# Pooled attention with a feed-forward layer: the maximum over partitions spread by one bfloat16 product, scales made straight from PSUM

## The chip, the cores and the metric

The kernel runs on one core of a Trainium2 chip, as one program. The metric is the device time of one execution in microseconds; lower is better. A core has a matrix engine (TensorE, PE), a vector engine (VectorE, DVE), an activation engine (ScalarE, ACT), a general engine (GpSimd, POOL) and a queue engine (SyncE, SP). They run side by side and meet through semaphores. TensorE writes to PSUM, an accumulator memory of 8 banks; the rest lies in SBUF. TensorE's weight loads are shown apart as PEld.

## The reference

There are 4 batches of 8 heads, 1152 positions and 64 values per head. Queries are averaged in pairs along the sequence, so that 576 query rows attend to 1152 keys. The result goes through a layer with normalisation and two products of 512 x 2048 and 2048 x 512.

```python
q_pool = q.reshape(B, H, S // 2, 2, D).mean(axis=3)
scores = scale * np.matmul(q_pool, k.transpose(0, 1, 3, 2))
scores = scores - np.max(scores, axis=-1, keepdims=True)
attn = np.exp(scores)
attn = attn / (np.sum(attn, axis=-1, keepdims=True) + 1e-09)
x = np.matmul(attn, v)          # then heads side by side: (4, 576, 512)
mu = np.mean(x, axis=-1, keepdims=True)
var = np.mean((x - mu) ** 2, axis=-1, keepdims=True)
xn = (x - mu) / np.sqrt(var + 1e-06) * g_ln
out = x + np.maximum(xn @ w_ch1, 0.0) @ w_ch2
```

All inputs and the output are float32.

## The kernel before

Two heads of one batch make a pair; there are 16 pairs, and each has 9 steps of 128 query rows (144 steps in all, `step(i)`). The order of the work is written out by hand: `step` emits for each engine what it does in step `i`, and a few queues (`reds`, `found`, `evacs`, `preps`, `units`, `calm`, and `todo` and `early` by step number) hold work that is slipped in between.

A float32 product is made out of float16 products: a matrix is scaled by a power of two and split into a high and a low float16 part. For this the kernel needs a bound of the largest absolute value of k, q and v of each pair and of each of four weight parts. `bound` (or `w_reduce` for weights) leaves one value on each of the 128 partitions; `all_max` makes the maximum over the partitions and spreads it to all of them; `scales` (or `w_scales`) makes powers of two out of it by masking exponent bits. All of this happens 20 times: once ahead of the first step, once for each of the pairs 1 to 15 (in step 3 of the pair before), and four times for weights.

`all_max` has two halves. `one` (L204) transposes the column of values, so that 1 to 3 rows of 128 values lie in PSUM; VectorE takes their maximum (L207) and puts it on the diagonal of a tiny matrix `dg` (L208). `two` (L215) multiplies a float32 matrix of ones of 3 rows by 128 columns with `dg`, so that each partition holds the maxima in PSUM. Then `scales` (L235 to L249) runs on VectorE: copy out of PSUM with a least bound TINY, mask the exponent (L240), mask and invert it (L241), multiply the inverse by 2^13 (L243), and make the product of two exponents `sc` (L245, L249). `w_scales` (L765 to L778) is the same for a weight part.

Steps 0 to 35 (batch 0, to about 186 us) transpose the exponentials on TensorE in float32 (`emit_t`, L431; `emit_t_copy`, L437) and multiply them in float32 (L455), while the weights are loaded and converted on VectorE (L103 in the profile). There `two` follows `emit_t` on TensorE, and what VectorE does with its result follows the step's maximum (L384). In the later steps (L365 and L373 are the scores, L467 the product with v, L619 and L651 the feed-forward products) the exponentials are split into `hl` (L412; the low part on VectorE, L421, or on GpSimd in every third step, L254 and L419) and transposed by DMA. There the results of `all_max` are taken in `flush`, in line with the other evacuations of PSUM: L516 and L517 (the sums of a row), L632 and L633 (the feed-forward's first layer: ScalarE writes the high part, VectorE the low part and frees the bank), L289 and L286 (the transposed k and q, which need the new scale `s`).

GpSimd adds the pairs of query rows (`pool_q`, L166) for two pairs at once, as soon as their DMA has landed; it also splits the weights (`w_split_a`, `_b`, `_c`: L254 and L797) and v (`take_v`).

The lines that a reader needs beside the functions printed below are these.

```python
# step(), steps of the first batch
emit_t(i)
if reds:
    found.append(reds.popleft()())
# step(), later steps
red = reds.popleft(); put = [None]
until([lambda: put[0]()])      # taken in the next flush()
...
put[0] = red()                 # after the product with v
```

Of the kernel before, what the change touches and what calls it, by code (L numbers as in the profile page):

```python
# [9 lines left out]
FP32 = mybir.dt.float32  # L10
FP16 = mybir.dt.float16
BF16 = mybir.dt.bfloat16
I32 = mybir.dt.int32
ACTF = mybir.ActivationFunctionType
ALU = mybir.AluOpType
# [3 lines left out]
EXPO = 0x7F800000  # L19
SIGN = -0x80000000  # L20
TINY = 2.0 ** -80
# [3 lines left out]
def tile_pooled_attention_moe(  # L25
# [18 lines left out]
    nc = tc.nc  # L44
# [18 lines left out]
    const = ctx.enter_context(tc.tile_pool(name="const", bufs=1))  # L63
# [5 lines left out]
    sm_p = ctx.enter_context(tc.tile_pool(name="sm", bufs=2))  # L69
# [4 lines left out]
    psum = ps_p.tile([128, 8, 512], FP32, name="psum")  # L74


    ident = const.tile([128, 128], FP32, name="ident")
# [3 lines left out]
    gsb = const.tile([128, KD], FP32, name="gsb")  # L81
    gs1 = const.tile([128, 2, KD], FP32, name="gs1")
    wtop = const.tile([128, 4, KD, 2], FP32, name="wtop")
    ones3 = const.tile([3, 128], FP32, name="ones3")
    wmax = const.tile([128, 4], FP32, name="wmax")
    wexp = const.tile([128, 4], FP32, name="wexp")
    wscl = const.tile([128, 4], FP32, name="wscl")
    inv12 = const.tile([128, 2], FP32, name="inv12")
    both = const.tile([128, 2], FP32, name="nhalf")
# [18 lines left out]
    def load(p, which, eng):  # L108
        b, hp = divmod(p, HP)
        h = 2 * hp  # L110
        src = k if which == "k" else v
        x = src[b, h:h + 2].rearrange("h (p c) d -> p h c d", c=C)
        if which == "k":
            r = raw_p.tile([128, 2, C + 1, D], FP32, tag="kr", name="kr")
            eng.dma_start(out=r[:, :, 0:C], in_=x)
            eng.dma_start(out=r[:, :, C], in_=x[:, :, C - 1])
        else:
            r = raw_p.tile([128, 2, C, D], FP32, tag="vr", name="vr")
            eng.dma_start(out=r, in_=x)
        raws[p, which] = r  # L120

    def load_q(p, engs, us=(0, 1)):

        if 0 in us:
            r = raw_p.tile([128, 2, C, 2, D], FP32, tag="qr", name="qr", bufs=2)
        else:
            r = raws[p, "q"]
        for u in us:
            b, hp = divmod(p + u, HP)
            for h in range(2):  # L130
                engs[(2 * u + h) % len(engs)].dma_start(
                    out=r[64 * u:64 * u + 64, h],
                    in_=q[b, 2 * hp + h].rearrange("(p c r) d -> p c r d", c=C, r=2),
                )
            raws[p + u, "q"] = r
# [3 lines left out]
    def state(p):  # L139
        if p not in pair:  # L140
            pair[p] = {
                x: sm_p.tile([128, 3], FP32, tag=x, name=x, bufs=3)
                for x in ("acc", "red", "e", "s", "sc")
            }
        return pair[p]

# [45 lines left out]

    def all_max(src, n, then):

        mx = sm_p.tile([3, 1], FP32, tag="mx3", name="mx3")
        dg = sm_p.tile([3, 3], FP32, tag="dg", name="dg")

        def place():
            u = this[0] if on_pe(this[0]) else pv_slot[0]
            return psum[:, 3 * (u % 2) + 2, 258:386]  # L200

        def one():
            ps = place()
            nc.tensor.transpose(ps[0:n], src, ident)  # L204

            def evac():
                nc.vector.tensor_reduce(mx[0:n], ps[0:n], axis=AX.X, op=ALU.max)  # L207
                nc.vector.scalar_tensor_tensor(  # L208
                    dg[0:n, 0:n], ps[0:n, 0:n], mx[0:n], ident[0:n, 0:n], op0=ALU.max, op1=ALU.mult
                )  # L210
            return evac

        def two():
            ps = place()
            nc.tensor.matmul(out=ps[:, 0:n], lhsT=ones3[0:n], rhs=dg[0:n, 0:n], start=True, stop=True)  # L215
            return lambda: then(ps[:, 0:n])

        return one, two


    reds, found = deque(), deque()

    def scales_reduce(p, a=0, b=3, then=None):
        def end(ps):
# [3 lines left out]

        reds.extendleft(reversed(all_max(pair[p]["acc"][:, a:b], b - a, end)))

    def scales(p, top, a=0, b=3, both=False):
        st = pair[p]
        red, e, s, sc = (st[x] for x in ("red", "e", "s", "sc"))
        v = nc.vector
        v.tensor_scalar(red[:, a:b], top, TINY, None, op0=ALU.max)  # L235
        if both:

            v.tensor_tensor(red[:, 0:1], red[:, 0:1], red[:, 2:3], op=ALU.max)
        ri, ei, si = (x.bitcast(I32)[:, a:b] for x in (red, e, s))
        v.tensor_scalar(ei, ri, EXPO, None, op0=ALU.bitwise_and)  # L240
        v.tensor_scalar(si, ri, EXPO, EXPO, op0=ALU.bitwise_and, op1=ALU.bitwise_xor)  # L241

        v.tensor_scalar(s[:, a:b], s[:, a:b], 2.0 ** 13, None, op0=ALU.mult)  # L243
        if a == 0:
            v.scalar_tensor_tensor(  # L245
                sc[:, 0:1], e[:, 0:1], 2.0 ** -32, e[:, 1:2], op0=ALU.mult, op1=ALU.mult
            )
            if on_pe(p * C):
                v.scalar_tensor_tensor(  # L249
                    sc[:, 1:2], e[:, 0:1], -(2.0 ** -32), e[:, 1:2], op0=ALU.mult, op1=ALU.mult  # L250
                )

    def scaled(dst, src, s=1.0):
# [85 lines left out]
    def on_pe(i):  # L339

        return 0 <= i < HP * C
# [196 lines left out]
    free_banks = [6, 7]  # L538
# [222 lines left out]

    def w_scales(part, top):
        w = part // 2
        m, e, s = wmax[:, part:part + 1], wexp[:, part:part + 1], wscl[:, part:part + 1]
        nc.vector.tensor_scalar(m, top, TINY, None, op0=ALU.max)  # L765
        mi = m.bitcast(I32)
        nc.vector.tensor_scalar(e.bitcast(I32), mi, EXPO, None, op0=ALU.bitwise_and)
        nc.vector.tensor_scalar(
            s.bitcast(I32), mi, EXPO, EXPO, op0=ALU.bitwise_and, op1=ALU.bitwise_xor
        )  # L770

        nc.vector.tensor_scalar(s, s, 2.0 ** (3 if part % 2 == 0 else 13), None, op0=ALU.mult)
        if part % 2 == 0:
            nc.vector.tensor_scalar(gs1[:, w], gsb, s, None, op0=ALU.mult)
        else:
            nc.vector.scalar_tensor_tensor(  # L778
                inv12[:, w:w + 1], wexp[:, part - 1:part], 2.0 ** -20, e,
                op0=ALU.mult, op1=ALU.mult,  # L780
            )

# [32 lines left out]
    for p in range(1, NP):  # L815
# [4 lines left out]
        if p % 2 == 0:  # L820
# [4 lines left out]
            else:  # L825
                x = i0 - (6 if p == 6 else 5)
# [234 lines left out]
    def warm(n, ps=None):  # L1061
        ps = psum[:, 2, 0:128] if ps is None else ps[:, 0:128]
        for _ in range(n):
            nc.tensor.matmul(out=ps, lhsT=ident16, rhs=ident16, start=True, stop=True)

    with tc.manual_schedule():
        def now(fn, *a, **k):
            fn(*a, **k)

        load_q(0, (nc.sync, nc.scalar), (0,))  # L1070
        load(0, "k", nc.sync)
        load(0, "v", nc.scalar)
        load_q(0, (nc.sync,), (1,))
        nc.sync.dma_start(out=gsb, in_=g_ln.rearrange("(k p) -> p k", p=128))
        nc.vector.memset(nhalf, -0.5)
        nc.vector.memset(both[:, 1:2], 0.0)
        nc.vector.memset(both[64:65, 1:2], 1e-9)
        nc.vector.memset(ones3, 1.0)
        nc.scalar.activation(out=wexp[:, 0:1], in_=nhalf, func=ACTF.Exp)
        make_identity(nc, ident)  # L1080

        warm(110)
        st = state(0)
        nc.vector.memset(st["acc"], 0.0)
        lower = (0, 64)
        pool_q(0, nc.vector, (lower,))
        dup_q(0, nc.gpsimd, (lower,))
        bound(0, "q", *lower)

        nc.scalar.activation(  # L1090
            out=kt_of(0).rearrange("p a h n -> p (a h n)")[:, 0:C * D],
            in_=raws[0, "k"][:, 0, 0:C].rearrange("p c d -> p (c d)"), func=ACTF.Abs,
            accum_out=st["acc"][:, 0:1],
        )
        nc.vector.tensor_reduce(
            st["acc"][:, 2:3], raws[0, "k"][:, 1, 0:C], axis=AX.XY, op=ALU.max,
            apply_absolute_value=True,
        )
        one, two = all_max(st["acc"], 3, lambda ps: scales(0, ps, 0, 3, both=True))
        one()()  # L1100
        two()()
        free_banks[:] = [6, 7, 3, 4, 5]
        parts = [fn(0, u) for fn, u in PREPS[:3]]
        for hi, lo in parts:
            hi()
            lo()
        warm(16)
        emit_s(0)
        preps.extend((fn, 0, u) for fn, u in PREPS[3:])
        free_banks[:] = [6, 7]  # L1110
        for h in range(2):
            take_v(0, h)
        i = 0
        while i < NSTEP + 20 or units or evacs or norms:
            step(i)
            i += 1
# [29 lines left out]
```

## Time and profile before

| what | value |
|---|---|
| time, median of 3 runs | 838.04 us (836.68 to 840.03) |
| span of the profiled execution | 836.1 us |
| PE busy | 808.8 us, 97% of the span |
| PEld busy | 575.8 us, 69% |
| DVE busy | 608.3 us, 73% |
| ACT busy | 558.0 us, 67% |
| POOL busy | 352.0 us, 42% |
| chain that ended last | PE 72%, DVE 10%, ACT 9%, DMA 4% |

The span runs from the first to the last instruction of one profiled execution. No time of its own is given for that execution beside the span; the three timed runs lie 0.6 to 3.9 us above it, their median 1.9 us. Busy time is what an engine spent in instructions. The chain follows the work that ended last back to what released each step. "Issue" in it is time in which an engine waited for nothing that the profile shows.

### The profile page before, as it was taken

Reading aid. Unit: us, or ns where it says so; the run is one execution under the profiler, and the core shown is the slowest. Engines: PE = TensorE matmul, PEld = TensorE weight load, DVE = VectorE, ACT = ScalarE, POOL = GpSimd, SP = SyncE. Lnnn points to the kernel's source line nnn. Section 1 sums busy time; section 2 is a strip of 40 time slices with the busy share of each in tenths; the row PEclk is TensorE's granted clock in tenths of the full one; section 3 lists DMA queues with packets and bytes.
Section 4 is the critical chain, followed back from the end, with each engine's and each line's share of the span. In section 5 each row is a group of like instructions: output and inputs, shape, how many; then the busy total and the mean of one; then the engine's idle time right before and its main releaser. Section 6 shows DMA issues by size and latency. Waiting matters only on the chain.

```text
span 836.1 us, 21671 instructions
## 1 busy us (share of the span) xinstructions
PE 808.8 (97%) x9142; PEld 575.8 (69%) x9142; DVE 608.3 (73%) x1167; ACT 558.0 (67%) x810; POOL 352.0 (42%) x343
## 2 busy tenths in 40 slices
PE   8999999998899989999999999999999999999997
PEld 6787887777566666767576766766666767667764
DVE  3598989899788888897887778888787877522221
ACT  3999988976787868787776777677867766211110
POOL 3020334287999972356452543636243432200000
PEclk9999999999999999999999999999999999999999
DMA  6954474115698989899979987996969867401001
GB/s 162 249 175 139 157 209 161 32 60 114 131 186 136 192 160 199 144 189 180 183 135 179 208 162 140 177 204 104 212 118 194 144 119 137 89 2 26 15 1 25
DMA packets 276018, 115.97 MB, mean 139 GB/s; under 512 B 259280, under 2 KB 259280, under 8 KB 275920
## 3 DMA queue, kind: packets, MB, share of 16 engines
q1 hardware_dynamic: 275568, 113.70, 66.0%
q8 instruction: 71, 1.16, 0.6%
q10 hardware_dynamic: 352, 0.88, 0.4%
q14 instruction: 27, 0.22, 0.1%
HBM read 46.14 MB, written 4.72 MB: 61 GB/s over the span
## 4 chain that ended last, share of the span: by engine, by line
PE 72%; DVE 10%; ACT 9%; DMA 4%; issue 3%; POOL 2%; SPq 1%; ACTq 0%; POOLq 0%; DVEq 0%
PE psum L651 21%; PE psum L619 21%; PE psum L467 10%; PE psum L365 8%; ACT pe L398 3%; PE psum L373 3%; DVE mx L384 3%; PE psum L455 2%; PE psum L328 2%; PE psum L431 2%; DVE hl L421 1%; PE psum L300 1%; ACT pt L437 1%; DMA kr<-in_k_dram 1%; DMA stage<-in_moe_w_ch_dram 1%
## 5 line engine op out<-in xcount | busy, mean ns | idle before, releaser
L384 DVE TENSOR_REDUCE mx<-psum 128x1 f32<-128x1152 f32 x144 | 194.3, 1349 | 16.4 <-PE psum L467 6.8
L398 ACT ACTIVATE pe<-psum,nb,sc 128x1152 f32<-128x1152 f32 x144 | 188.5, 1309 | 21.8 <-POOL hl L419 9.3
L651 PE MATMUL psum<-wsl,ht 128*128 128x512 f16 x864 | 196.7, 379 | 0.2 <-ACT pe L398 0.2
L619 PEld LDWEIGHTS <-wsl 128*128 128x128 f16 x1920 | 170.7, 98 | 23.2 <-issue 3.9
L619 PE MATMUL psum<-xn,wsl 128*128 128x256 f16 x1536 | 179.0, 275 | 3.5 <-DVE ht L633 2.3
L651 PEld LDWEIGHTS <-ht 128*128 128x128 f16 x864 | 80.5, 98 | 88.3 <-issue 0.2
L365 PE MATMUL psum<-kt,qt 64*128 64x512 f16 (+1 forms) x960 | 127.2, 380 | 4.8 <-ACT pe L398 4.5
L632 ACT ACTIVATE ht<-psum 128x512 f16<-128x512 f32 x72 | 42.9, 596 | 132.3 <-PE psum L619 132.1
L412 ACT ACTIVATE hl<-pe 128x1152 f16<-128x1152 f32 x108 | 125.6, 1163 | 3.4
L467 PE MATMUL psum<-vt,pt 128*128 128x65 f16 (+1 forms) x3240 | 117.7, 194 | 0.4 <-DMA pt<-hl 0.2
L421 DVE SCALAR_TENSOR_TENSOR hl<-pe,hl 128x1152 f16<-128x1152 f32 x72 | 112.2, 1559 | 0.0
L467 PEld LDWEIGHTS <-pt 128*128 128x128 f16 (+1 forms) x3240 | 109.2, 100 | 3.3 <-DMA pt<-hl 0.7
L254 POOL TENSOR_SCALAR pe<-pe 128x1152 f32<-128x1152 f32 x36 | 43.4, 1205 | 142.1 <-ACT hl L412 142.1
L633 DVE SCALAR_TENSOR_TENSOR ht<-psum,ht 128x512 f16<-128x512 f32 x72 | 49.6, 689 | 73.6 <-ACT ht L632 73.6
L419 POOL TENSOR_TENSOR hl<-pe,hl 128x1152 f16<-128x1152 f32 x36 | 85.5, 2374 | 3.0
L455 PE MATMUL psum<-pt,vt 128*65 128x128 f32 (+1 forms) x720 | 77.3, 262 | 1.0 <-DVE qt L286 1.0
L455 PEld LDWEIGHTS psum<-pt,vt 128*65 128x65 f32 x720 | 71.6, 138 | 1.1 <-DVE qt L286 1.1
L365 PEld LDWEIGHTS <-qt 64*128 64x128 f16 (+1 forms) x960 | 39.7, 96 | 42.5 <-issue 25.9
L373 PEld LDWEIGHTS <-qt 128*128 128x128 f16 (+1 forms) x320 | 17.1, 99 | 62.0 <-issue 61.8
L286 DVE SCALAR_TENSOR_TENSOR qt<-psum,s,qt 128x384 f16<-128x384 f32 x48 | 29.5, 615 | 34.8 <-ACT qt L289 34.6
L260 POOL COPY gate<-gate 128x1 f32<-128x1 f32 x27 | 5.2, 191 | 111.0 <-DVE gate L259 111.0
L665 DVE SCALAR_TENSOR_TENSOR xb<-psum,inv,xb 128x512 f32<-128x512 f32 x32 | 23.8, 745 | 36.9 <-PE psum L651 36.8
(117 smaller groups left out, 1025.7 us busy)
## 6 DMA issues: line engine op xcount, KB each, us to landing
stage<-in_moe_w_ch_dram SPq DMA_DIRECT2D x32, 512.0 KB, 5.8
kr<-in_k_dram SPq DMA_DIRECT2D x16, 576.0 KB, 4.4
qr<-in_q_dram SPq DMA_DIRECT2D x31, 288.0 KB, 6.0
vr<-in_v_dram SPq DMA_DIRECT2D x15, 576.0 KB, 4.8
out_dram<-xb SPq DMA_DIRECT2D x32, 128.0 KB, 2.5
pt<-hl SPq DMA_TRANSPOSE x108, 4.9
kr<-in_k_dram SPq DMA_DIRECT2D x16, 64.0 KB, 4.1
vr<-in_v_dram ACTq DMA_DIRECT2D x1, 576.0 KB, 7.6
```

The lines of the kernel that those rows point to most:

```text
L254: nc.gpsimd.tensor_scalar(dst, src, s, 1.0, op0=ALU.mult, op1=ALU.mult)
L365: nc.tensor.matmul(out=sp[o:o + w, c0:c0 + 512], lhsT=qt[r:r + 64, qa, q0:q0 + w], rhs=kt[r:r + 64, ka, h], start=(a == 0), stop=(a == 2),)
L384: nc.vector.tensor_reduce(mx, st["s"], axis=AX.X, op=ALU.max)
L398: nc.scalar.activation(out=st["pe"], in_=st["s"], func=ACTF.Exp, scale=pair[i // C]["sc"][:, 0:1], bias=st["nb"],)
L412: nc.scalar.activation(out=hl[:, 0], in_=st["pe"], func=ACTF.Copy, scale=2.0 ** 15)
L419: nc.gpsimd.tensor_tensor(hl[:, 1], st["pe"], hl[:, 0], op=ALU.subtract)
L421: nc.vector.scalar_tensor_tensor(hl[:, 1], st["pe"], 2.0 ** 15, hl[:, 0], op0=ALU.mult, op1=ALU.subtract)
L455: nc.tensor.matmul(out=ps[0:65, q0:q0 + w], lhsT=vt[:, h, c], rhs=pt[:, 128 * u + q0:128 * u + q0 + w], start=(u == 0), stop=(u == C - 1),)
L467: nc.tensor.matmul(out=dst[:, 0:n], lhsT=lhsT, rhs=rhs, start=(u == 0 and lhsT is hi and n == 65), stop=(u == C - 1 and lhsT is lo), skip_ ...
L619: nc.tensor.matmul(out=ps[:, o:o + n], lhsT=wsl[:, 8 * w + cc, wa, f * 128:f * 128 + 128], rhs=xn[:, xa * KD + cc, 0:n], start=(m == 0), s ...
L633: lambda: nc.vector.scalar_tensor_tensor(lo, pv, 0.0, hi, op0=ALU.max, op1=ALU.subtract),
L651: nc.tensor.matmul(out=ps, lhsT=hv[0][:, ha, f, t * 128:t * 128 + 128], rhs=wsl[:, 8 * w + 4 + f // 2, wa, (f % 2) * DM:(f % 2) * DM + DM] ...
```

## The change

`two` multiplies a bfloat16 matrix of 128 x 128 equal values (2^-13) with a bfloat16 matrix `dg` of 128 rows, of which all but the diagonal of the first rows is zero. `dg` is one of four places of a constant tile that is zeroed once. The least bound TINY is written once into one PSUM column (386) of banks 2 and 5, next to the 128 columns that `one` fills, and L207 reduces 129 columns. `scales` and `w_scales` mask exponents straight out of PSUM; the copy with TINY and the multiplication by 2^13 are gone, their factors are in other constants. Ahead of the first step the maximum of two parts of k is taken before the transpose, not after it.

```diff
-    ones3 = const.tile([3, 128], FP32, name="ones3")
+    ones = const.tile([128, 128], BF16, name="ones")
+    diag = const.tile([128, 4, 4], BF16, name="diag")
...
     def all_max(src, n, then):
         mx = sm_p.tile([3, 1], FP32, tag="mx3", name="mx3")
-        dg = sm_p.tile([3, 3], FP32, tag="dg", name="dg")
+        diags[0] += 1
+        dg = diag[:, diags[0] % 4]
         def place():
             u = this[0] if on_pe(this[0]) else pv_slot[0]
-            return psum[:, 3 * (u % 2) + 2, 258:386]
+            return psum[:, 3 * (u % 2) + 2, 258:387]
         def one():
             ps = place()
-            nc.tensor.transpose(ps[0:n], src, ident)
+            nc.tensor.transpose(ps[0:n, 0:128], src, ident)
...
         def two():
             ps = place()
-            nc.tensor.matmul(out=ps[:, 0:n], lhsT=ones3[0:n], rhs=dg[0:n, 0:n], start=True, stop=True)
+            nc.tensor.matmul(out=ps[:, 0:n], lhsT=ones, rhs=dg[:, 0:n], start=True, stop=True)
             return lambda: then(ps[:, 0:n])
...
-    def scales(p, top, a=0, b=3, both=False):
+    def scales(p, top, a=0, b=3):
         st = pair[p]
-        red, e, s, sc = (st[x] for x in ("red", "e", "s", "sc"))
+        e, s, sc = (st[x] for x in ("e", "s", "sc"))
         v = nc.vector
-        v.tensor_scalar(red[:, a:b], top, TINY, None, op0=ALU.max)
-        if both:
-            v.tensor_tensor(red[:, 0:1], red[:, 0:1], red[:, 2:3], op=ALU.max)
-        ri, ei, si = (x.bitcast(I32)[:, a:b] for x in (red, e, s))
-        v.tensor_scalar(ei, ri, EXPO, None, op0=ALU.bitwise_and)
-        v.tensor_scalar(si, ri, EXPO, EXPO, op0=ALU.bitwise_and, op1=ALU.bitwise_xor)
-        v.tensor_scalar(s[:, a:b], s[:, a:b], 2.0 ** 13, None, op0=ALU.mult)
+        ei, si = (x.bitcast(I32)[:, a:b] for x in (e, s))
+        ti = top.bitcast(I32)
+        v.tensor_scalar(ei, ti, EXPO, None, op0=ALU.bitwise_and)
+        v.tensor_scalar(si, ti, EXPO, EXPO, op0=ALU.bitwise_and, op1=ALU.bitwise_xor)
         if a == 0:
             v.scalar_tensor_tensor(
-                sc[:, 0:1], e[:, 0:1], 2.0 ** -32, e[:, 1:2], op0=ALU.mult, op1=ALU.mult
+                sc[:, 0:1], e[:, 0:1], 2.0 ** -6, e[:, 1:2], op0=ALU.mult, op1=ALU.mult
             )
...
     def w_scales(part, top):
         w = part // 2
-        m, e, s = wmax[:, part:part + 1], wexp[:, part:part + 1], wscl[:, part:part + 1]
-        nc.vector.tensor_scalar(m, top, TINY, None, op0=ALU.max)
-        mi = m.bitcast(I32)
-        nc.vector.tensor_scalar(e.bitcast(I32), mi, EXPO, None, op0=ALU.bitwise_and)
+        e, s = wexp[:, part:part + 1], wscl[:, part:part + 1]
+        ti = top.bitcast(I32)
+        nc.vector.tensor_scalar(e.bitcast(I32), ti, EXPO, None, op0=ALU.bitwise_and)
         nc.vector.tensor_scalar(
-            s.bitcast(I32), mi, EXPO, EXPO, op0=ALU.bitwise_and, op1=ALU.bitwise_xor
+            s.bitcast(I32), ti, EXPO, EXPO, op0=ALU.bitwise_and, op1=ALU.bitwise_xor
         )
-        nc.vector.tensor_scalar(s, s, 2.0 ** (3 if part % 2 == 0 else 13), None, op0=ALU.mult)
         if part % 2 == 0:
-            nc.vector.tensor_scalar(gs1[:, w], gsb, s, None, op0=ALU.mult)
+            nc.vector.tensor_scalar(gs1[:, w], gsb, s, 2.0 ** -10, op0=ALU.mult, op1=ALU.mult)
...
-        nc.vector.memset(ones3, 1.0)
+        for n in (2, 5):
+            nc.vector.memset(psum[:, n, 386:387], TINY)
+        nc.vector.memset(diag, 0.0)
+        nc.vector.memset(ones, 2.0 ** -13)
...
-        one, two = all_max(st["acc"], 3, lambda ps: scales(0, ps, 0, 3, both=True))
+        nc.vector.tensor_tensor(st["acc"][:, 0:1], st["acc"][:, 0:1], st["acc"][:, 2:3], op=ALU.max)
+        one, two = all_max(st["acc"][:, 0:2], 2, lambda ps: scales(0, ps, 0, 2))
         one()()
         two()()
-        free_banks[:] = [6, 7, 3, 4, 5]
+        free_banks[:] = [6, 7, 3, 4]
```

## Rows read from the trace of the kernel before

**Rows 1.** The page: busy time, and the chain that ended last by engine.

```profile
PE 808.8 (97%) x9142; PEld 575.8 (69%) x9142; DVE 608.3 (73%) x1167; ACT 558.0 (67%) x810; POOL 352.0 (42%) x343
...
PE 72%; DVE 10%; ACT 9%; DMA 4%; issue 3%; POOL 2%; SPq 1%; ACTq 0%; POOLq 0%; DVEq 0%
```

**Rows 2.** The chain that ended last, near 252 us: start, length, engine, tile, line.

```profile
251.85 0.82 PE psum L467 x27
252.67 0.31 PE psum L215 x2
```

**Rows 3.** The same chain from 38 to 43 us, in the first batch.

```profile
38.26 0.31 PE psum L215 x2
...
39.53 0.17 DVE red L235
...
39.73 0.17 DVE e L240
...
40.30 0.09 DVE r L514
...
43.01 1.29 DVE mx L384
```

**Rows 4.** Timeline near 298 us: start, length, engine, line, operation, idle before.

```profile
296.28 2.61 POOL L166 TENSOR_TENSOR qr<-qr 128x1152 f32<-128x1152 f32 x1 [3.96 <-DMA qr<-in_q_dram]
296.30 0.15 DVE L235 TENSOR_SCALAR red<-psum 128x3 f32<-128x3 f32 x1
296.49 2.43 DVE L240 TENSOR_SCALAR e<-red 128x3 int32<-128x3 int32 x1
...
297.11 0.60 ACT L632 ACTIVATE ht<-psum 128x512 f16<-128x512 f32 x1 [1.63 <-PE psum L619]
...
298.71 0.99 PE L467 MATMUL psum<-vt,pt 128*128 128x65 f16 x27 [0.23 <-DMA pt<-hl]
...
298.85 2.12 POOL L797 TENSOR_TENSOR wsl<-wsl 128x1024 f16<-128x1024 f32 x1
299.02 2.04 DVE L243 TENSOR_SCALAR s<-s 128x3 f32<-128x3 f32 x1
...
301.30 0.67 DVE L633 SCALAR_TENSOR_TENSOR ht<-psum,ht 128x512 f16<-128x512 f32 x1
...
302.03 4.43 PE L619 MATMUL psum<-xn,wsl 128*128 128x256 f16 x24 [2.33 <-DVE ht L633]
```

**Rows 5.** Stretches: length, busy time (count) of PE, PEld, DVE, ACT, POOL, granted clock, DMA.

```profile
298.70:302.00 3.30, 0.99 (x27) 0.90 (x28) 3.23 (x8) 0.84 (x2) 3.09 (x4) 1.00 0.99 204
302.00:304.00 2.00, 1.97 (x10) 1.38 (x10) 2.00 (x3) 1.97 (x2) 1.90 (x2) 0.50 0.88 164
```

**Rows 6.** Timeline near 471 us, PE: the same group of products elsewhere.

```profile
470.97 2.79 PE L619 MATMUL psum<-xn,wsl 128*128 128x256 f16 x24
```

**Rows 7.** Timeline near 564 us: a wait of PE behind the scales.

```profile
558.64 3.31 DVE L421 SCALAR_TENSOR_TENSOR hl<-pe,hl 128x1152 f16<-128x1152 f32 x1
...
562.33 0.17 DVE L243 TENSOR_SCALAR s<-s 128x3 f32<-128x3 f32 x1
...
562.59 0.69 ACT L289 ACTIVATE kt<-psum,s 128x512 f16<-128x512 f32 x1 [1.99 <-DVE s L243]
...
564.21 0.63 PE L574 MATMUL psum<-ident,xs 128*128 128x128 f32 x4 [1.47 <-DVE kt L286]
```

**Rows 8.** Timeline near 129 us, GpSimd's and VectorE's: a scale of a weight part.

```profile
128.19 2.13 POOL L797 TENSOR_TENSOR wsl<-wsl 128x1024 f16<-128x1024 f32 x1
...
129.80 0.53 DVE L778 SCALAR_TENSOR_TENSOR inv<-wexp 128x1 f32<-128x1 f32 x1
```

**Rows 9.** Timeline of the first scales, ahead of step 0.

```profile
12.14 0.16 DVE L238 TENSOR_TENSOR red<-red 128x1 f32<-128x1 f32 x1
...
13.03 0.69 ACT L289 ACTIVATE kt<-psum,s 128x512 f16<-128x512 f32 x1 [2.66 <-PE psum L300]
```

**Rows 10.** Source view of L166 in the later steps: count, ns min/median/max, first and last start.

```profile
L166 POOL TENSOR_TENSOR qr<-qr x5: 2614/2619/2638, 203.7 to 558.1; 128x1152 f32<-128x1152 f32 x5
```

More of the change, by code (lines that the diff above doesn't have):

```diff
@@ L142, in state @@
                 x: sm_p.tile([128, 3], FP32, tag=x, name=x, bufs=3)
-                for x in ("acc", "red", "e", "s", "sc")
+                for x in ("acc", "e", "s", "sc")
             }
@@ L214, in two @@
             ps = place()
-            nc.tensor.matmul(out=ps[:, 0:n], lhsT=ones3[0:n], rhs=dg[0:n, 0:n], start=True, stop=True)
+            nc.tensor.matmul(out=ps[:, 0:n], lhsT=ones, rhs=dg[:, 0:n], start=True, stop=True)
             return lambda: then(ps[:, 0:n])
         return one, two
-    reds, found = deque(), deque()
+    reds, found, diags = deque(), deque(), [0]
     def scales_reduce(p, a=0, b=3, then=None):
@@ L249, in scales @@
                 v.scalar_tensor_tensor(
-                    sc[:, 1:2], e[:, 0:1], -(2.0 ** -32), e[:, 1:2], op0=ALU.mult, op1=ALU.mult
+                    sc[:, 1:2], e[:, 0:1], -(2.0 ** -6), e[:, 1:2], op0=ALU.mult, op1=ALU.mult
                 )
@@ L763, in w_scales @@
         w = part // 2
-        m, e, s = wmax[:, part:part + 1], wexp[:, part:part + 1], wscl[:, part:part + 1]
-        nc.vector.tensor_scalar(m, top, TINY, None, op0=ALU.max)
-        mi = m.bitcast(I32)
-        nc.vector.tensor_scalar(e.bitcast(I32), mi, EXPO, None, op0=ALU.bitwise_and)
+        e, s = wexp[:, part:part + 1], wscl[:, part:part + 1]
+        ti = top.bitcast(I32)
+        nc.vector.tensor_scalar(e.bitcast(I32), ti, EXPO, None, op0=ALU.bitwise_and)
         nc.vector.tensor_scalar(
-            s.bitcast(I32), mi, EXPO, EXPO, op0=ALU.bitwise_and, op1=ALU.bitwise_xor
+            s.bitcast(I32), ti, EXPO, EXPO, op0=ALU.bitwise_and, op1=ALU.bitwise_xor
         )
-        nc.vector.tensor_scalar(s, s, 2.0 ** (3 if part % 2 == 0 else 13), None, op0=ALU.mult)
         if part % 2 == 0:
-            nc.vector.tensor_scalar(gs1[:, w], gsb, s, None, op0=ALU.mult)
+            nc.vector.tensor_scalar(gs1[:, w], gsb, s, 2.0 ** -10, op0=ALU.mult, op1=ALU.mult)
         else:
             nc.vector.scalar_tensor_tensor(
-                inv12[:, w:w + 1], wexp[:, part - 1:part], 2.0 ** -20, e,
+                inv12[:, w:w + 1], wexp[:, part - 1:part], 2.0 ** 6, e,
                 op0=ALU.mult, op1=ALU.mult,
```

## The prediction

> **What bounds the kernel now.** I read the page first: PE is busy 97% of the span, and the chain that ended last is 72% PE [rows 1]. So a cut elsewhere counts only where something else stands last. I then followed the chain in order of time past the 20 places where a maximum is spread, and the timeline wherever PE stood idle there. The reader should see three patterns.
>
> In the later steps PE does one group after another, and the product of L215 is one link of that chain, 0.31 us long: it is float32, so two weight loads and two passes stand there [rows 2]. In the first batch the chain goes through L215 and then through VectorE: the scales begin at 39.53, the next line begins at 40.30, and VectorE stays last up to the step's maximum at 43.01 [rows 3]. There VectorE, though not the busiest engine, is the late one.
>
> The third pattern is a single place. At 296.28 GpSimd starts L166, which takes 2.61 us. VectorE's L235, which reads PSUM, runs beside it in its usual 0.15 us; L240, which reads and writes SBUF, takes 2.43 us and ends when L166 ends. GpSimd's next, L797, then holds L243 in the same way for 2.04 us. All that VectorE has behind them waits: L633, which frees a bank, runs at 301.30 instead of after L632 at 297.71, and PE stands idle for 2.33 us [rows 4]. The granted clock was 1.00 until then and 0.50 (1.2 GHz) after that idle time [rows 5], and the group of L619 takes 4.43 us [rows 4] where it takes 2.79 us elsewhere [rows 6].
>
> **The change part by part.** The sum is made against the profiled span, 836.1 us; the median of the runs, 838.04, lies 1.9 us above it.
>
> (a) *The product.* It becomes one weight load and one pass. The trace has no lone bfloat16 pair of this size. From below, a float16 pair of L467 costs 0.82 us / 27 = 0.03 us in a row of such pairs; from above, it costs what it does now, 0.31 [rows 2]. I take 0.08, near the float16 pair because it is the same kind of load and pass, but above it because a lone pair has nothing like it before or behind it. That saves 0.23. Such a piece of 0.31 stands on the chain 12 times: seven times in the later steps, as in [rows 2], five in the first batch, as in [rows 3]; at the other eight another engine or a DMA is last. 12 x 0.23 = 2.8 us; between 0 and 12 x 0.28 = 3.4.
>
> (b) *Two VectorE instructions less per scale.* In the first batch the chain runs through the scales six times. L240 can start only 0.20 us after L235, whose result it reads (39.53 to 39.73 in [rows 3]); the copy and the multiplication by 2^13 each put one such step into the chain, so 2 x 0.20 = 0.40 us of the 0.77 goes. 6 x 0.40 = 2.4 us. If something else is at once as late (ScalarE's copies run beside it), it is 0; more than 2.6 is not in it. In the later steps these cuts lie beside PE's groups and are worth nothing, except at (c) and (d). Reading PSUM instead of SBUF costs nothing here, as L235 at 0.15 against the usual 0.17 of L240 shows [rows 3].
>
> The Trainium skill ("VectorE: DVE Perf Modes", section "Why PSUM operands drop a tier") speaks against this part: with a PSUM operand a float32 instruction loses the fast mode that uses both read ports. At two or three values per partition the rows show no price for that; by the rule it is what lets go of GpSimd in (c).
>
> (c) *The stall at 296 us.* L240 and L241 will read PSUM and, like L235 in [rows 4], not wait for GpSimd; L243 is gone. What is late next is L245, which multiplies two SBUF columns. The trace has a twin of it: L778, two SBUF columns of the same shape, took 0.53 us at 129.80 and ended with GpSimd's L797 [rows 8], where L238, with two SBUF columns too, took 0.16 [rows 9]. So I expect L245 to wait for the end of L166 at 298.89 and then go ahead of L797, as L240 did. In [rows 4] PE starts 0.97 us after L243 has ended at 301.06; after L245 has ended, about 299.0, it takes the same, so L619 could start at 299.95. L467 ends at 299.70: PE idles 0.25 in place of 2.33. It had just waited 0.23 for a DMA [rows 4], at a granted clock of 1.00 [rows 5], so the clock should stay. That gives 2.33 + (4.43 - 2.79) - 0.25 = 3.7 us. If L245 doesn't wait, L633 follows L632 at 297.71 and PE doesn't idle: 4.0. If L245 stays behind L797 too, up to 300.97, nothing is gained: 0. I take 3.7.
>
> The Trainium skill ("SBUF — State Buffer", section "Who interferes with whom") has the same rule: a VectorE instruction with two SBUF inputs contends with a GpSimd instruction that reads SBUF, as one in a two-port mode does, and the one that comes second is fully blocked. By it L245 is held like its twin in [rows 8], 3.7; without it the term would be 4.0.
>
> (d) *The scales near 562 us.* L421 is held there by another L166, then the scales run, ScalarE waits 1.99 us for L243 and PE in the end 1.47 [rows 7]. `s` will be ready with the second instruction instead of the fourth: 0.4 us earlier, and so is PE. Bounds 0 and 0.6.
>
> (e) *Ahead of step 0.* A maximum of 0.16 us (L238's length) moves ahead of the transpose, and (a) gives 0.23 back; behind it ScalarE waits for PE's transposes of k, not for the scales [rows 9]. Net 0, within 0.2 either way. The new fills run while VectorE waits for the first queries; without that cover they would cost less than 0.3 us, an estimate from L235's 0.15 for two instructions as small. One column more in L207, and four places for `dg` in place of two, cost nothing: no wait for `dg` shows past the first.
>
> Sum: 2.8 + 2.4 + 3.7 + 0.4 = 9.3 us. Span 836.1 - 9.3 = 826.8; with 1.9 for what lies around it, 828.7 us. No DMA, queue or loop moves, so nothing new stands in the way of SP or POOL.
>
> **The rivals.**
>
> *The wait stays.* L797 goes ahead of L245, or the timed runs, which lie 3.35 us apart, have the stall of (c) in only some executions. For it: L797 starts at 298.85, right at L166's end, and L243 did wait for it. Against: L240, already waiting, got in first [rows 4]. Then (c) is 0 and the rest stands: 838.04 - 5.6 = 832.4 us.
>
> *The small cuts are hidden.* In the first batch PE, ScalarE and VectorE are nearly level, so taking 0.6 us from one of a step's links leaves the others; in the later steps the 0.23 of PE turns into waits for the DMA of `pt`, of which 0.23 at 298.71 is a sample [rows 4]. For it: that sample. Against: the chain shows VectorE without a gap from 39.53 to 43.01 [rows 3] and PE without one near 252 [rows 2]. Then only (c) counts, 834.3 us; if the wait stays as well, 838.0, no change.
>
> *The product gains nothing.* A weight load of 128 rows in place of 3, and the wait for `dg` in front of it, might cost what the float32 product does. Against: both loads have 128 columns. Then 831.5 us.
>
> *Slower.* L166 comes five times in the later steps [rows 10]. Its start follows a DMA, not VectorE's order, so it meets whatever VectorE is doing. With the scales shorter, L421 and L245, which read two SBUF operands, slide into it more often. Once PE is late by more than its slack, one meeting costs what [rows 4] shows, 3.97 us with the clock's fall. It decides from the third further meeting on: four more, at the other four poolings, give 838.04 - 5.6 + 4 x 3.97 = 848.3 us. For it: at 558.64 L421 was held for 2 us [rows 7]. Against: that cost PE 1.47 without (c)'s chain of two, and the scales themselves become harder to hold.
>
> **How the numbers follow.** About 0.5% (4.2 us) is what a measurement of this kernel can tell from no change. Forecast 0.49 (826 to 832); the wait stays 0.15; cuts hidden 0.09, with the wait as well 0.13; product gains nothing 0.06; slower 0.08. Under 833.85 lie the forecast, the wait that stays and the product without gain, 0.70; I take off 0.08 for mixes in which part of (a) and (b) is hidden too: 0.62 for faster. Those 0.07 and the cuts hidden in both forms, 0.22, make 0.29 within 0.5%; slower gets 0.08 and 0.01 of the mixes, 0.09. The range runs down to 825.5: all upper bounds, 3.4 + 2.6 + 4.0 + 0.6 = 10.6, give 827.4, less 1.4 for the scatter of the runs below their median and 0.5 for (e) and what I don't see. It runs up to 838.5, which takes in no change and leaves out the slower case and the thin ends.
>
> **What the profile after would show.** L215 once per spread, near 0.1 us on PE's part of the chain; if 0.3, (a) is wrong. Scales of 0.35 us where 0.77 stood, in the first batch; if the step's maximum doesn't come earlier, (b) is wrong. At about 296 us the masks at 0.15 us beside L166; L245 long, up to 2.4 us, then L633 at once, PE idle under 0.5 us, and a granted clock of 1.00 up to 306 us; if the clock falls there, (c) is wrong. A second place of clock 0.50 in the later steps, behind L421 or L245, would speak for the slower rival.

## The result and the profile after

The changed kernel takes 828.88 us (median of 4 runs, 827.00 to 830.28) against 837.36 us (835.40 to 840.03): a ratio of 0.9893, 95% interval 0.9871 to 0.9915. It is faster, by about 8.5 us where 9.3 were forecast. Its profiled span is 825.2 us against 836.1. The page of the changed kernel, busy time and the chain by engine, against [rows 1]:

```profile
PE 798.8 (97%) x9122; PEld 568.5 (69%) x9122; DVE 603.1 (73%) x1130; ACT 558.8 (68%) x810; POOL 354.9 (43%) x343
...
PE 72%; DVE 9%; ACT 9%; DMA 4%; issue 3%; POOL 2%; SPq 1%; ACTq 0%; POOLq 0%; DVEq 0%
```

PE has 20 products less (9122 for 9142) and 10 us less busy time; it is still the bound. Part of the 10 us is the clock: two of its falls (at 11.9 and 302.0 us) are missing in the trace after, and the one at 302 alone cost 1.64 us (4.43 for 2.79, [rows 4, 6]). The product, now L218, in the chain that ended last near 248 us, where [rows 2] stood before:

```profile
247.91 0.82 PE psum L466 x27
248.73 0.00 PE psum L218
248.73 2.64 PE psum L618 x24
```

The link of 0.31 us is gone. In the first batch, against [rows 3], the chain no longer turns to VectorE behind the product:

```profile
36.12 0.99 PE psum L430 x9
37.11 0.00 PE psum L218
37.11 0.12 PE psum L482
37.23 1.97 PE psum L454 x18
39.19 0.44 PE psum L299 x4
```

Near 292 us (timeline: start, length, engine, line), against [rows 4]:

```profile
291.76 2.63 POOL L167 TENSOR_TENSOR qr<-qr 128x1152 f32<-128x1152 f32 x1 [3.74 <-DMA qr<-in_q_dram]
...
292.00 0.15 DVE L241 TENSOR_SCALAR e<-psum 128x3 int32<-128x3 int32 x1
292.06 0.15 DVE L242 TENSOR_SCALAR s<-psum 128x3 int32<-128x3 int32 x1
...
292.18 2.22 DVE L244 SCALAR_TENSOR_TENSOR sc<-e 128x1 f32<-128x1 f32 x1
...
294.34 2.14 POOL L791 TENSOR_TENSOR wsl<-wsl 128x1024 f16<-128x1024 f32 x1
...
294.64 0.67 DVE L632 SCALAR_TENSOR_TENSOR ht<-psum,ht 128x512 f16<-128x512 f32 x1
...
295.37 2.78 PE L618 MATMUL psum<-xn,wsl 128*128 128x256 f16 x24 [0.22 <-DVE ht L632]
```

The masks run beside GpSimd's L167 (L166 before) in 0.15 us. The product of exponents, L244, is held until L167 ends and then goes ahead of L791. PE idles 0.22 us and the group of L618 takes its usual 2.78. The granted clock stays at 1.00 (stretches, as in [rows 5]):

```profile
295.40:297.90 2.50, 2.50 (x24) 2.24 (x24) 2.50 (x3) 1.84 (x3) 2.50 (x3) 1.00 0.95 177
```

To see where time went, I measured profiled executions between the starts of the same steps' maxima (L384 in [rows 3], one per step): ahead of step 0, steps 3 to 36 (the first batch), 36 to 58, 58 to 63 (the stall), 63 to 143, and the span. All in us, worked out from the traces; "again" and "third" are further executions, and the other rows are the experiments below:

```
                        step 0   3 to 36  36 to 58  58 to 63  63 to 143   span
before                  16.74    154.39   106.00    29.39     388.73     836.1
before, again           15.98    154.37   105.98    27.24     388.57     832.9
after                   15.58    151.53   105.83    25.44     386.03     825.2
after, again            17.47    151.45   106.93    25.75     386.78     829.2
after, third            15.34    151.48   105.83    25.22     385.65     824.3
product alone           17.21    152.72   106.75    25.51     387.70     830.7
scales alone            16.59    153.38   107.35    25.04     389.66     832.8
one multiplication gone 17.65    153.73   105.89    28.74     388.47     835.3
masks by column         15.98    154.88   107.22    25.56     390.86     835.3
product twice           17.41    155.51   107.55    27.49     392.44     841.2
before, sum later       16.15    154.39   104.69    25.85     388.20     830.0
```

The first batch repeats within 0.1 us for one kernel; the other stretches don't, and step 0 differs by 2 us between executions of the changed kernel alone. The experiments say why.

### The profile page after: what moved, and what is told of

Same layout as the page of the kernel before. It is cut to its first block, busy times and chain, and to the rows that moved or that the text cites. A ratio compares the mean times of both kernels' runs of the same rounds, so it can differ in the third digit from the quotient of the medians.

```text
span 825.2 us, 21594 instructions
## 1 busy us (share of the span) xinstructions
PE 798.8 (97%) x9122; PEld 568.5 (69%) x9122; DVE 603.1 (73%) x1130; ACT 558.8 (68%) x810; POOL 354.9 (43%) x343
## 4 chain that ended last, share of the span: by engine, by line
PE 72%; DVE 9%; ACT 9%; DMA 4%; issue 3%; POOL 2%; SPq 1%; ACTq 0%; POOLq 0%; DVEq 0%
PE psum L650 21%; PE psum L618 20%; PE psum L466 10%; PE psum L364 9%; PE psum L454 3%; ACT pe L397 3%; PE psum L372 3%; PE psum L430 2%; DVE mx L383 2%; DMA kr<-in_k_dram 2%; PE psum L327 2%; DVE hl L420 2%; PE psum L299 1%; ACT pt L436 1%; DMA stage<-in_moe_w_ch_dram 1%
## 5 line engine op out<-in xcount | busy, mean ns | idle before, releaser
L618 PEld LDWEIGHTS <-wsl 128*128 128x128 f16 x1920 | 169.4, 98 | 20.2 <-issue 2.3
L618 PE MATMUL psum<-xn,wsl 128*128 128x256 f16 x1536 | 176.3, 273 | 1.8 <-DVE qt L285 0.8
L420 DVE SCALAR_TENSOR_TENSOR hl<-pe,hl 128x1152 f16<-128x1152 f32 x72 | 113.2, 1573 | 0.0
```

Of the source, the lines that this page charges most:

```text
L420: nc.vector.scalar_tensor_tensor(hl[:, 1], st["pe"], 2.0 ** 15, hl[:, 0], op0=ALU.mult, op1=ALU.subtract)
L618: nc.tensor.matmul(out=ps[:, o:o + n], lhsT=wsl[:, 8 * w + cc, wa, f * 128:f * 128 + 128], rhs=xn[:, xa * KD + cc, 0:n], start=(m == 0), s ...
```

## The experiments

**The product alone.** The kernel before with the new product and nothing else of the change.

```diff
+        dg = diag[:, diags[0] % 4]
...
-            nc.tensor.matmul(out=ps[:, 0:n], lhsT=ones3[0:n], rhs=dg[0:n, 0:n], start=True, stop=True)
+            nc.tensor.matmul(out=ps[:, 0:n], lhsT=ones, rhs=dg[:, 0:n], start=True, stop=True)
...
+        nc.vector.memset(ones, 1.0)
```

> The kernel before with the bfloat16 product alone: 128 rows of ones, dg in bfloat16, while the copy with TINY, the masks out of SBUF and the multiplication by 2^13 stay. My theory, three causes that add up: the product is worth 2.8 us, so 837.4 - 2.8 = 834.6; L215 is one load and one pass of under 0.1 us on PE's chain, and the stall near 296 us stays, with PE idle for some 2.3 us and a granted clock of 0.50 behind it. Rival, the stall is all that counts: 837.4, no change. Rival, the product is all that counts: 829.

Measured: 832.97 against 837.18 us, ratio 0.9953 (0.9938 to 0.9969), 2.6 to 5.2 us. More than 2.8 at the median, less than all. But the stall did not stay as I had said. Near 295 us (timeline):

```profile
295.41 0.17 DVE L242 TENSOR_SCALAR e<-red 128x3 int32<-128x3 int32 x1
...
295.49 0.16 DVE L243 TENSOR_SCALAR s<-red 128x3 int32<-128x3 int32 x1
295.55 2.61 POOL L167 TENSOR_TENSOR qr<-qr 128x1152 f32<-128x1152 f32 x1 [4.53 <-DMA qr<-in_q_dram]
...
295.69 2.51 DVE L245 TENSOR_SCALAR s<-s 128x3 f32<-128x3 f32 x1
...
298.12 2.13 POOL L799 TENSOR_TENSOR wsl<-wsl 128x1024 f16<-128x1024 f32 x1
...
299.22 2.78 PE L621 MATMUL psum<-xn,wsl 128*128 128x256 f16 x24 [0.16 <-DVE ht L635]
```

Here the masks started 0.06 to 0.14 us before GpSimd's instruction, so only the multiplication was held, once, and nothing behind L799 (L797 before). PE idled 0.16. The stall needs two holds in a row, and the landing of a DMA decides by tenths of a us whether there are two.

The same trace has a fall of the clock that the kernel before does not have (timeline, then a stretch):

```profile
558.24 0.63 PE L576 MATMUL psum<-ident,xs 128*128 128x128 f32 x4 [2.03 <-DVE kt L288]
...
561.10 3.77 PE L653 MATMUL psum<-wsl,ht 128*128 128x512 f16 x12
```

```profile
559.75:563.10 3.35, 3.35 (x34) 2.09 (x32) 3.32 (x6) 2.57 (x3) 0.12 (x1) 0.50 0.13 25
```

In the kernel before this group (L651 there) takes 2.75 us, and the group of L469 ahead of it 0.98 where it is 1.61 here: the fall cost 1.6 us. Steps 63 to 143 are 1.0 us shorter as they stand in the table, and would be 2.7 shorter without it.

**The scales alone.** The changed kernel with the float32 product put back.

```diff
-            nc.tensor.matmul(out=ps[:, 0:n], lhsT=ones, rhs=dg[:, 0:n], start=True, stop=True)
+            nc.tensor.matmul(out=ps[:, 0:n], lhsT=ones3[0:n], rhs=dg[0:n, 0:n], start=True, stop=True)
...
+        nc.vector.memset(ones3, 2.0 ** -13)
```

> The changed kernel with the float32 product of 3 rows put back (its ones are 2^-13), so that only the scales out of PSUM and the TINY column are left of the change. Three causes: 2.4 (two VectorE instructions in the first batch) + 3.7 (the stall) + 0.4 = 6.5 us, so 830.9; beside L166 the masks take 0.15 us, the product of exponents is held for about 2.2 us, PE idles under 0.5 us and its clock stays at 1.00. Rival, the product is all that counts: 837.4.

Measured: 834.41 us, ratio 0.9959 (0.9945 to 0.9974): 3.4 us, not 6.5. In the table, steps 58 to 63 show the whole gain (25.04), but the first batch only 1.0 us of the 2.4, and 63 to 143 a loss of 0.9: PE waited 1.02 us for a DMA of `pt` at 382.79. Steps 36 to 58 are 1.4 us longer; the fall of the clock near 210 us lasts twice as long there as in the kernel before (6.8 us for 3.4). No scale was held near 296 us, because L166 started just after the product of exponents; so this trace has the gain, but not the masks beside GpSimd (timeline):

```profile
296.20 0.16 DVE L242 SCALAR_TENSOR_TENSOR sc<-e 128x1 f32<-128x1 f32 x1
...
296.28 2.62 POOL L166 TENSOR_TENSOR qr<-qr 128x1152 f32<-128x1152 f32 x1 [4.25 <-DMA qr<-in_q_dram]
```

**One multiplication gone.** As the last, with the copy kept, so that the masks read SBUF.

```diff
+        v.tensor_scalar(st["red"][:, a:b], top, TINY * 2.0 ** -13, None, op0=ALU.max)
-        ti = top.bitcast(I32)
+        ti = st["red"].bitcast(I32)[:, a:b]
```

> As the run with the float32 product and the scales out of PSUM, but the copy with TINY from PSUM to SBUF is put back ahead of the masks, so that the masks read SBUF again and only the multiplication by 2^13 is gone. Three causes: the first mask is held by L166 to its end, as before, but nothing is held behind L797, so PE idles about 0.25 us and the stall's 3.7 us are gained all the same; of the 2.4 us of the first batch half is left: 837.4 - 3.7 - 1.2 - 0.2 = 832.3. Rival, the stall goes only when the masks read PSUM: PE idles over 2 us, the clock falls, 836.

Measured: 836.69 us, ratio 0.9993 (0.9975 to 1.0011). The rival was right, though not for its reason (timeline near 297 us):

```profile
296.69 1.76 DVE L240 TENSOR_SCALAR e<-red 128x3 int32<-128x3 int32 x1
...
298.39 2.13 POOL L791 TENSOR_TENSOR wsl<-wsl 128x1024 f16<-128x1024 f32 x1
...
298.49 2.04 DVE L243 SCALAR_TENSOR_TENSOR sc<-e 128x1 f32<-128x1 f32 x1
...
301.50 4.45 PE L617 MATMUL psum<-xn,wsl 128*128 128x256 f16 x24 [2.00 <-DVE ht L631]
```

Once the mask is held, the product of exponents comes 0.10 us after L791 has started and is held behind it in the multiplication's place. Taking out one instruction doesn't help while another that can be held stands behind it.

**Masks by column.** The kernel before, each mask and multiplication as one instruction per column.

```diff
-        v.tensor_scalar(ei, ri, EXPO, None, op0=ALU.bitwise_and)
+        for c in range(b - a):
+            v.tensor_scalar(ei[:, c:c + 1], ri[:, c:c + 1], EXPO, None, op0=ALU.bitwise_and)
...
```

> The kernel before, but in the scales of a pair each mask and the multiplication by 2^13 run as one instruction per column, 128 x 1, from SBUF to SBUF as before (6 or 3 more instructions per pair). What holds VectorE behind GpSimd, if it is a mode that needs two columns or more: the single-column masks take 0.15 to 0.17 us beside L166, the product of two columns is held instead, PE idles under 0.5 us near 296 us, and with 0.2 us more in each pair of the first batch the time is 837.4 - 3.7 + 0.6 = 834.3. Rival, every instruction from SBUF to SBUF is held: one of the masks takes over 2 us and one more is held behind L797, PE idles over 2 us, the clock falls, 838.

Measured: 838.15 us, ratio 1.0013 (0.9999 to 1.0028). The time is the rival's. Steps 58 to 63 gained 3.8 us (25.56), but as much was lost elsewhere: 0.5 in the first batch, 1.2 in steps 36 to 58 and 2.1 in 63 to 143, where PE waited 1.68 us for a DMA of `pt` at 384.30. That the six or three more instructions cost all of it is not shown. The mechanism is the theory's: near 297 us the masks began just before L166, but near 472 us they ran in the middle of it (timeline):

```profile
470.82 2.62 POOL L166 TENSOR_TENSOR qr<-qr 128x1152 f32<-128x1152 f32 x1 [5.21 <-DMA qr<-in_q_dram]
...
472.15 0.28 DVE L241 TENSOR_SCALAR e<-red 128x1 int32<-128x1 int32 x3
472.35 0.26 DVE L243 TENSOR_SCALAR s<-red 128x1 int32<-128x1 int32 x3
...
472.72 0.74 DVE L249 SCALAR_TENSOR_TENSOR sc<-e 128x1 f32<-128x1 f32 x1
```

Nine single columns from SBUF to SBUF weren't held; the product of two columns was, to L166's end.

**Both kernels once more.**

> The kernel before, another execution with a profile. My theory by now: the stall near 296 us is a meeting in time. It needs two holds in a row, a mask behind L166 and a second instruction behind L797, and L166 starts when a DMA lands, a few tenths of a us to either side of the masks. So the stall of 3.9 us with the clock's fall is in some executions and not in others; where it is missing, PE idles under 0.5 us (or waits about 1 us for the DMA of pt) near 298 us. Rival: it is fixed by the order of the work; then it is there again, with PE idle over 2 us and a granted clock of 0.50.

> The changed kernel, another execution with a profile. If the scales out of PSUM can be held only once (the product of exponents behind L166), no execution has the fall of the clock near 295 us. Rival: that product can also stay behind L797; then PE idles about 2 us there in some executions. The fall of the clock ahead of step 0, near 12 us, should be in some executions of either kernel, since it was missing in the first profile of this one and in the one with masks by column, and there in the other four.

The kernel before took 834.70 us in that run, the changed one 830.98; single runs, so their traces count. Neither expectation for the kernel before held whole: the two holds were there again, but not the clock's fall (timeline, then a stretch):

```profile
295.75 1.87 DVE L240 TENSOR_SCALAR e<-red 128x3 int32<-128x3 int32 x1
...
297.72 2.04 DVE L243 TENSOR_SCALAR s<-s 128x3 f32<-128x3 f32 x1
...
300.73 2.78 PE L619 MATMUL psum<-xn,wsl 128*128 128x256 f16 x24 [2.17 <-DVE ht L633]
```

```profile
300.70:303.00 2.30, 2.27 (x21) 2.04 (x21) 2.30 (x3) 2.27 (x3) 2.20 (x2) 1.00 0.79 150
```

So the stall cost 1.8 us there (58 to 63: 27.24 against 25.44 after, one cheaper product included) and 3.9 where the clock fell (29.39). The changed kernel again had one hold there (L244, 2.43 us; PE idle 0.29) and no fall. It met GpSimd elsewhere: L420 held for 2.3 us, and PE idle 1.04 (timeline):

```profile
464.03 2.63 POOL L167 TENSOR_TENSOR qr<-qr 128x1152 f32<-128x1152 f32 x1 [3.44 <-DMA qr<-in_q_dram]
464.19 3.68 DVE L420 SCALAR_TENSOR_TENSOR hl<-pe,hl 128x1152 f16<-128x1152 f32 x1
...
470.62 2.75 PE L650 MATMUL psum<-wsl,ht 128*128 128x512 f16 x12 [1.04 <-DVE ht L632]
```

The fall ahead of step 0 (granted clock 0.50 from 11.3 to 18 us) came in one of the two, and the other way round than in the first pair: it belongs to neither kernel.

**The product twice.** The kernel before with L215 issued twice, a dose.

```diff
+            nc.tensor.matmul(out=ps[:, 0:n], lhsT=ones3[0:n], rhs=dg[0:n, 0:n], start=True, stop=True)
```

> The kernel before with each float32 product of L215 issued twice, one behind the other, into the same place. It measures the price of one such product by a dose: if each is a link of PE's chain of 0.31 us at 12 of the 20 places, as I predicted, 837.4 + 12 x 0.31 = 841.1; at 16 places 842.4. Rival, the small cuts and costs are hidden by what is as late: 837.4 to 838.5.

Measured: 840.18 against 837.09 us, ratio 1.0037 (1.0021 to 1.0054), 1.8 to 4.5 us. The second one is 0.22 us on the chain near 255 us:

```profile
255.23 0.31 PE psum L215 x2
255.54 0.22 PE psum L216 x2
```

The product is a link that counts; a dose of 0.22 at 12 to 16 places is 2.6 to 3.5 us.

**GpSimd's sum a step later,** in the kernel before and in the changed one.

```diff
-                x = i0 - (6 if p == 6 else 5)
+                x = i0 - 4
```

> The kernel before, but the sum of query pairs on GpSimd (L166) is emitted a step later (for the pair near 203 us two steps later), behind the split of weights (L797) and the low part (L254, L419) that stand behind it now; nothing of the scales is changed. Theory of two holds: L797 runs while the DMA is still on its way, only L166 can hold the masks, PE idles under 0.5 us near 298 us and the clock stays: 3.7 us in the executions that have the stall. Near 205 us the low part no longer waits for the DMA of the queries, so PE's wait of 4.1 us and the fall of the clock behind it (1.7) go too: 837.2 - 5 - (0 to 3.7) = 828.5 to 832. Rival, GpSimd's order doesn't matter because the DMA sets everything: 837.

> The changed kernel with the same later place of L166. Theory: at 292 us only the product of exponents is held by L166, as now, no gain; near 204 us PE's wait of 4.5 us and the clock's fall go: 828.9 - 5 = 823.9. Rival, GpSimd's order doesn't matter: 828.9.

Measured: before 834.19 us, ratio 0.9958 (0.9943 to 0.9974); changed 825.96 us, ratio 0.9862 (0.9833 to 0.9890), both to the kernel before. In the kernel before (timeline), with the scales as they were:

```profile
290.32 2.14 POOL L797 TENSOR_TENSOR wsl<-wsl 128x1024 f16<-128x1024 f32 x1
...
294.26 2.62 POOL L166 TENSOR_TENSOR qr<-qr 128x1152 f32<-128x1152 f32 x1 [1.80 <-DMA qr<-in_q_dram]
...
295.29 1.69 DVE L240 TENSOR_SCALAR e<-red 128x3 int32<-128x3 int32 x1
...
297.02 0.17 DVE L243 TENSOR_SCALAR s<-s 128x3 f32<-128x3 f32 x1
...
298.22 2.78 PE L619 MATMUL psum<-xn,wsl 128*128 128x256 f16 x24 [0.85 <-DVE ht L633]
```

L797 now runs while the DMA is on its way, so one hold is left; 58 to 63 takes 25.85 us. The stall is GpSimd's order and VectorE's scales together, and either end mends it. PE's wait of 4.1 us near 212 us also went, but other waits came (1.24 at 237.69), and the clock fell behind them after all (granted 0.50 from 239.7 us; in the changed kernel's version from 213.3), so 3.5 us were gained, less than I said.

**One pair later; and the last held instruction put off.** The changed kernel again (third execution), with `x = i0 - 5` for the pair near 203 us alone, and with `x = i0 - 4` and the product of exponents in the next flush.

```diff
+        if on_pe(p * C):
+            product()
+        else:
+            until([product])
```

> The changed kernel once more, to stand beside the versions of this call on the same chip: 828.9 (827 to 831).

> The changed kernel with L166's work emitted one step later for the third pair of its kind alone (the one near 203 us), all others as they were. If the gain of the version with all of them later came from PE's wait of 4.5 us near 208 us, this one has it too: about 826. If it came from the others, 828.9.

> The changed kernel with L166's work later for all pairs and, in the later steps, the product of two exponents (the one instruction of the scales that reads two SBUF columns) put off to the next flush. Theory: at about 291 us nothing of the scales is held by L166; PE's remaining wait of 0.2 to 0.5 us there goes. Against the version without the delay (825.96): 825.5, not to be told from it by time; the trace tells. Rival: the delayed product is held in its new place and holds the first-layer low part there: 826 to 828.

Measured, on one chip: 827.97 (ratio 0.9883, 0.9855 to 0.9912), 825.69 (0.9859, 0.9833 to 0.9886) and 830.36 us (0.9914, 0.9890 to 0.9937). The intervals of the first two overlap, so that the version beats the changed kernel is likely and not shown; in its profile PE's wait near 208 us fell from 4.5 to 2.27. In the changed kernel's third execution L244 began 0.05 us before L167 (291.74 and 291.79) and took 0.16 us: no hold at all. The version with the product put off fell to its rival: the product was put into the way of another GpSimd instruction, at three of the pairs in the same manner (timeline):

```profile
336.51 2.36 POOL L423 TENSOR_TENSOR hl<-pe,hl 128x1152 f16<-128x1152 f32 x1
...
336.85 2.04 DVE L244 SCALAR_TENSOR_TENSOR sc<-e 128x1 f32<-128x1 f32 x1
...
339.85 2.75 PE L655 MATMUL psum<-wsl,ht 128*128 128x512 f16 x12 [1.66 <-DVE ht L637]
```

## Why the prediction was right

The sum was right, 9.3 forecast and 8.5 measured at the medians (by the interval 7.1 to 10.8), and each of the three main mechanisms is there. That the sum came so near is partly luck: (a) gave about 1.6 us more than its term, (b) about 1.3 less, (d) nothing, and (c) from half of its term to a little more, by the execution.

(a) The product: right in kind, sized too small. In the run with the product alone the first batch is 1.67 us shorter for its seven spreads; I had put 5 x 0.23 there. Steps 63 to 143, with eight spreads, are 2.7 us shorter when the fall of the clock near 560 us is taken off. Together 4.4, forecast 2.8 in all; that the two stretches as they stand also give 2.7 is luck. The link of 0.31 goes whole (0.00 is left), not by 0.23, and 4.4 us is 14 such links. PE's busy time in steps 63 to 143 says the same: 385.2 to 385.3 us with the float32 product (before, before again, scales alone), 382.0 to 382.2 in the changed kernel's three executions, and 383.6 with the product alone, the fall's 1.6 in it. So where the changed kernel is 2.0 to 3.1 us shorter in these steps, it is the product's doing and not the scales'. The run with the product alone measured 3.9 us; in its profiled execution the double hold was missed, and how often in the other eleven no trace shows.

(b) Two VectorE instructions less: right in kind, sized too large. The step that failed is that the whole 0.40 us stays on the chain. The scales alone gave 1.0 us in the first batch, and 1.2 on top of the product (152.72 against 151.53); forecast 2.4. Behind the first tenths PE is as late as VectorE, as the chain from 36 to 39.6 us shows, now PE without a gap: of the six places of the first batch at which the chain ran through the scales, two are left in the changed kernel and in the run with the scales alone. My own rival had said so for all small cuts; it held for this one by half.

(c) The stall: the mechanism was right to the instruction in the first profile (L244 held 2.22 us, PE idle 0.22 for 0.25, clock kept). Its price was the profiled execution's, not the usual one. Of the four executions with two holds (before, before again, one multiplication gone, product twice) two had the clock's fall; the gain is 1.8 us without it and 3.9 with it. Forecast 3.7.

The Trainium skill ("SBUF — State Buffer", section "Who interferes with whom") has it that a VectorE instruction with two SBUF inputs is blocked by a GpSimd instruction that reads SBUF and was issued first; L244's 2.22 us agrees, and so does the delayed product's 2.04.

(d) The scales near 562 us: 0.4 us forecast, nothing gained. The scales did shorten: ScalarE's L288 starts 0.24 us after the end of L420, where L289 started 0.64 after the end of L421. But L420 began 0.17 us behind L167, not 0.55, and was held longer, so that PE idles 1.84 us for 1.47; in the other two executions of the changed kernel it idles 1.41 and 1.47 (timeline, against [rows 7]; first GpSimd's instruction in the kernel before, then the changed kernel):

```profile
558.09 2.64 POOL L166 TENSOR_TENSOR qr<-qr 128x1152 f32<-128x1152 f32 x1 [1.16 <-DMA qr<-in_q_dram]
```

```profile
548.46 2.65 POOL L167 TENSOR_TENSOR qr<-qr 128x1152 f32<-128x1152 f32 x1 [1.52 <-DMA qr<-in_q_dram]
548.63 3.68 DVE L420 SCALAR_TENSOR_TENSOR hl<-pe,hl 128x1152 f16<-128x1152 f32 x1
...
552.55 0.69 ACT L288 ACTIVATE kt<-psum,s 128x512 f16<-128x512 f32 x1 [1.95 <-DVE s L242]
...
554.17 0.63 PE L573 MATMUL psum<-ident,xs 128*128 128x128 f32 x4 [1.84 <-DVE kt L285]
```

(e) Ahead of step 0: 0 forecast. The first profiles differ by 1.2 us, but by the clock, which falls there in some executions of each kernel. Where it fell in neither (before again, after), 0.4 us are left, 0.6 with the third execution of the changed kernel; I had allowed 0.2.

Of the rivals, the slower one's mechanism was seen: a further meeting once (L420 at 464 us), with PE idle for 1.04 us, and a longer hold at one meeting that was there before (near 549 us). Neither brought a fall of the clock. That the wait stays was not seen in the changed kernel's three traces.

## What to carry to other kernels

Ask of a tiny instruction not how long it takes but what can hold it and what stands behind it: a mask and a multiplication of 0.17 us each cost PE 2 to 4 us, because a bank waited behind them. When one engine holds another, count the holds in a row; taking out one instruction gained nothing while the next could be held in its place, and moving the holder mended the stall as changing the held did (steps 58 to 63: 25.85 and 25.04 us). And price a stall from several profiles: one execution's stall may have a fall of the clock in it that half the others don't have. The same holds for an experiment's gain, as the fall near 560 us in the run with the product alone shows.

## What the runs showed of the hardware

- VectorE's tensor_scalar instructions from SBUF to SBUF were held by GpSimd with three columns (2.43 and 2.04 us), not with one (0.26 to 0.28 us for three of them in the middle of L166), and not out of PSUM (0.15 us).
- When GpSimd's instruction ended, the waiting VectorE instruction went before GpSimd's next one. What came after that next one had started was held by it: in the kernel before, L241 at 298.83 us, 0.02 ahead of L797, took its usual 0.15 us, and L243, 0.17 behind L797's start, 2.04.
- PE idle for 2.33, 2.00 and (product alone, near 558 us) 2.03 us was followed by a granted clock of 0.50 (1.2 GHz); idle for 2.17 us, and for 2.37 in the run with the product twice, was not. In the kernel before with the sum a step later, waits of 1.24 and 0.57 us near 238 us were followed by such a fall too. What decides it no run shows.
- A lone bfloat16 product of 128 x 128 by 3 columns left no time of its own on PE's chain, where the float32 one left 0.31 us.
